# Attention, a routed expert layer and a dense layer in one kernel: another order in the attention, a shorter compaction, x first for the first expert, and other costs in the planner

## The chip, the cores and the metric

The kernel runs on one core of one Trainium2 chip. The metric is the device time of one execution in microseconds. Five engines work in order, each on its own queue: PE multiplies matrices and transposes, DVE, ACT and POOL work elementwise, and SP issues transfers; POOL issues the indirect ones. Data comes from DRAM into on-chip memory, and matmul results lie in PSUM, of which there are eight banks.

## The reference

```python
# 1. attention: B, H, S, D = 4, 8, 768, 64; chunks of 32 queries see 8 memory keys,
#    16 keys to the left, their own 32 and 8 to the right
scores = scale * q_c @ k_full.T
a = exp(scores - max(scores)); a = a / (sum(a) + 1e-09)
out[:, :, c_start:c_end] = a @ v_full
# 2. routed experts: N, D, E, F = 3072, 512, 8, 1024; cap = N // E = 384 tokens each
logits = x @ w_gate
for idx in argsort(-logits.flatten()):       # best pair of token and expert first
    if token is free and expert has room: assigned[tok] = e
for e in range(E):
    out[assigned == e] = max(x[assigned == e] @ w1[e], 0) @ w2[e]
# 3. dense: h = x @ w_in; solu = h * softmax(h); layer norm with gain g_ln; @ w_out
```

All is in float32. Each float32 product of the second and third part is made of three matmuls on a high and a low half (names ending in h and l).

## The kernel before

**Attention** (`attention`, lines 61 to 235) goes over 24 tiles of 128 queries for all 8 heads. Per tile `score` fills `s` with 32 matmuls (the page counts them so, the order lists 16 calls), DVE takes the row maximum `mx`, `less` writes `p` = s - mx, `expo` takes the exponential on ACT, `sums` adds up and inverts on DVE and scales on POOL, `trans` transposes p into `pt`, `pv` multiplies with the values into `o`, which ACT copies to `xs`, and `xtrans` transposes that for the gate. Loads run ahead of it in rings: five tiles of keys `kd` and queries `qt`, four of values `vd`. The keys and values go into block patterns, so the rings are cleared first. `gate` makes the logits `L` of four tiles at a time.

**Routing** (`Route.rounds`, lines 668 to 765) finds one expert per round: `search` finds a threshold in eight counting steps (24 small matmuls `r<-oh,ge`, then `r<-some,ones`, each answered by DVE), then the round picks the expert (`flags`, `es`, `iw`), ranks its tokens (`mk`, `slot`), packs their numbers into `idx` (`compact`, lines 767 to 819: one-hots `ohl` and `rhs`, 24 matmuls, the copy `cc`, four replicating matmuls), and masks the assigned ones in L. Round 0 has nothing beside it; the later ones run beside the experts.

**Experts** (`Experts.run`, lines 1104 to 1187). For each: POOL gathers three x tiles (`xg`) by idx and the weights (`raw`) by `iw`; PE transposes x (`tp<-ident,xg`), ACT and DVE split it into `xh` and `xl`; `g12` makes h = x w1 and y = h w2 in eight steps f of 12 + 12 matmuls; `g3` multiplies with the dense `in` matrix, 72 matmuls, called G3 here; `g4` with `out`, 72 matmuls, G4, one expert later. Beside this, `Fixed` splits the dense weights in chunks of 512 columns (tiles `v`, `e`, `in_h`, `in_l`, `out_h`, `out_l`), on ACT, DVE and POOL.

**What sets the order.** All engines work in program order, and the order is made when the program is built: `Pace` keeps one estimated clock per engine, advanced by `cost` and `charge` for every recorded instruction. The main line of PE work is written straight down; side jobs (routing, splits, chunks) are generators that `tick` resumes when their time has come by these clocks, or, with `yield "spare", "dve"`, when that engine's clock is not ahead of PE's by more than an allowance, less `fit` before another job's due time. So a different cost or `FIT` moves side jobs among the main rows. All instructions are recorded through one helper, so that the profile gives them one line, L398.

Of the kernel before, what the change touches and what calls it, by code (L numbers as in the profile page):

```python
# [42 lines left out]
FIRST_A = 3  # L43
SPARE = 1.27
FIT = 0.34
FIT_OUT = 0.27
# [8 lines left out]
def warm(nc, p, ident, n):  # L55

    for i in range(n):
        nc.tensor.transpose(p[:, i % 4], ident, ident)


def attention(nc, tc, q, kx, vx, wgx, ident, x_dram, L, consts, beside):

    with ExitStack() as ctx:
# [13 lines left out]
        def load_kq(i):  # L77
            if i < NT:
                for h2 in range(2):
                    nc.sync.dma_start(KD[i % AHEAD][h2::2, h2], kx[i, h2])  # L80
                nc.sync.dma_start(QT[i % AHEAD], q[i])
# [6 lines left out]
        for i in range(AHEAD):  # L88
            (nc.gpsimd if i % 2 else nc.vector).memset(KD[i], 0.0)
            if i < AHEAD - 1:  # L90
                (nc.vector if i % 2 else nc.gpsimd).memset(VD[i], 0.0)
# [6 lines left out]
        consts()  # L98

        warm(nc, ps.tile([128, 4, 128], F32, tag="t", name="warm"), ident, 20)  # L100
# [78 lines left out]
        def gate(u, js=range(4)):  # L179
            if js[0] == 0:  # L180
                G[u] = ps.tile([128, 128], F32, tag="t", name="g")
# [5 lines left out]
            if js[-1] == 3:  # L187
                g, G[u] = G[u], wk.tile([128, 128], F32, tag="gs", name="gs", bufs=2)
                nc.scalar.copy(G[u], g)

        def gate_last(i):

            g = ps.tile([128, 4, 128], F32, tag="t", name="g")[:, 0, 0:E]
# [4 lines left out]
        def gate_t(u):  # L198
            g = ps.tile([128, 4, 32], F32, tag="t", name="g")
            nc.tensor.transpose(g, G.pop(u), ident)  # L200
            nc.vector.tensor_scalar(L[:, 4 * u:4 * u + 4, :], g[:, :, 0:E], 0.0, None, op0=ALU.add)

        for i in range(NT + 5):
            n = 0
# [26 lines left out]
            if i > NT:  # L231
                gate_last(i - 5)
            if NT + 1 >= i >= 6 and (i - 6) % 4 == 3:
                gate_t((i - 6) // 4)
            beside(i, 4)


class Pace:
# [61 lines left out]
    def cost(self, eng, op, outs, ins, kw):  # L300
# [3 lines left out]
        if eng == "dve":  # L304
            return n / (1920 if op == "tensor_scalar" else 960) + 0.07
        if eng == "act":
            return n / 1200 + 0.09 + (0.15 if len(outs) > 1 or op == "activation" and n > 512 else 0.0)
        if eng == "pool":
            return n / (480 if op == "tensor_tensor" else 960) + 0.15
        t = (0.108 if op == "transpose" else max(0.03, 0.06 * n / 128) if kw.get("tile_position") else  # L310
             max(0.025, n / 2400 + 0.003))
# [4 lines left out]
    def charge(self, eng, op, args, kw):  # L316
# [8 lines left out]
        if "dma" in op:  # L325
            self.clk[eng] = start + (1.04 if eng == "pool" else 0.05)
# [193 lines left out]
class Route:  # L520
# [6 lines left out]
    def __init__(self, ctx, nc, tc, L, beside):  # L527
# [4 lines left out]
        self.held, self.stage = False, 0  # L532

    def consts(self, ident):
        nc, k = self.nc, self.k
# [8 lines left out]
        self.tri = k.tile([128, 128], F16, name="tri")  # L544
        V.tensor_scalar(self.tri, self.row, col, None, op0=ALU.is_gt)
# [4 lines left out]
        for i in range(3):  # L550
            V.tensor_scalar(self.jtab[:, i], self.jtab[:, 3], float(16 ** (3 - i)), None, op0=ALU.mult)
        off = iota(self.w.tile([128, 8, E], F32, tag="oh", name="off"), [[-15, 8], [0, E]], 0, 1)
        self.own = k.tile([128, 8, E], F16, name="own")
        up = self.w.tile([128, 8, E], F32, tag="rhs", name="up")
        V.tensor_scalar(up, off, 0.0, None, op0=ALU.is_ge)
        V.scalar_tensor_tensor(self.own, off, 15.0, up, op0=ALU.is_lt, op1=ALU.mult)
        V.tensor_tensor(up, self.own, off, op=ALU.mult)
# [707 lines left out]
```

## Time and profile before

| | |
|---|---|
| median of 3 runs | 783.28 us (783.23 to 784.56) |
| the profiled execution | 785.33 us, its span 783.6 us |
| PE busy | 715.6 us, 91% of the span |
| DVE busy | 528.2 us, 67% |
| ACT, POOL busy | 335.9 us, 43%; 199.2 us, 25% |
| chain that ended last | PE 72%, DVE 17%, waits on issue 3%, ACT 3%, DMA 2% |

The span is that of the instructions on the core; the execution's own time is 1.73 us longer. The slices of the page show three stretches: up to 118 us the attention, with PE between six and nine tenths; from 118 to 153 us a stretch in which PE is little used and its granted clock falls to 0.5; and from there on PE at nine tenths. A busy PE can still be slow, since a matmul's duration overlaps the next one's: the distance of two starts says what one costs.

### The profile page before, as it was taken

Reading aid. Unit: us, or ns where it says so; the run is one execution under the profiler, and the core shown is the slowest. Engines: PE = TensorE matmul, PEld = TensorE weight load, DVE = VectorE, ACT = ScalarE, POOL = GpSimd, SP = SyncE. Lnnn points to the kernel's source line nnn. Section 1 sums busy time; section 2 is a strip of 40 time slices with the busy share of each in tenths; the row PEclk is TensorE's granted clock in tenths of the full one; section 3 lists DMA queues with packets and bytes.
Section 4 is the critical chain, followed back from the end, with each engine's and each line's share of the span. In section 5 each row is a group of like instructions: output and inputs, shape, how many; then the busy total and the mean of one; then the engine's idle time right before and its main releaser. Section 6 shows DMA issues by size and latency. Waiting matters only on the chain.

```text
span 783.6 us, 14636 instructions
## 1 busy us (share of the span) xinstructions
PE 715.6 (91%) x5760; PEld 616.5 (79%) x5760; DVE 528.2 (67%) x1434; ACT 335.9 (43%) x646; POOL 199.2 (25%) x263
## 2 busy tenths in 40 slices
PE   6988784499989999999999999999999999999993
PEld 5766674378869978988898789888988898899882
DVE  7788866589997986972897289639964852553150
ACT  1565550234374354432742273237324632563170
POOL 5234530432441134004101420232023211410121
PEclk8999995689999999999999999999999999999997
DMA  7999873532360044004400430152015110600100
GB/s 252 343 323 331 320 286 132 202 103 60 110 227 1 1 162 131 5 1 147 150 1 17 160 120 1 36 181 81 1 55 188 55 40 28 220 10 1 40 14 27
DMA packets 30020, 89.35 MB, mean 114 GB/s; under 512 B 4224, under 2 KB 4352, under 8 KB 29952
## 3 DMA queue, kind: packets, MB, share of 16 engines
q0 software_dynamic: 13056, 46.14, 17.3%
q1 hardware_dynamic: 16896, 42.28, 15.6%
q8 instruction: 45, 0.74, 0.4%
q14 instruction: 23, 0.19, 0.1%
HBM read 75.83 MB, written 12.58 MB: 113 GB/s over the span
## 4 chain that ended last, share of the span: by engine, by line
PE 72%; DVE 17%; issue 3%; ACT 3%; DMA 2%; POOL 1%; POOLq 0%; DVEq 0%; ACTq 0%
PE h L398 32%; PE y L398 16%; PE o L398 15%; PE tp L398 4%; PE r L398 3%; DVE e L398 3%; DVE sum L398 2%; DMA xg<-x_dram,idx 2%; DVE p L398 2%; DVE mx L398 1%; DVE ge L398 1%; ACT p L398 1%; DVE w1l L398 1%; PE xtp L398 1%; PE g L398 1%
## 5 line engine op out<-in xcount | busy, mean ns | idle before, releaser
L398 PE MATMUL y<-hh,w2h 128*128 128x384 f32 x256 | 91.6, 358 | 7.9 <-DVE e L398 7.9
L398 PE MATMUL y<-hl,w2h 128*128 128x384 f32 x256 | 88.3, 345 | 0.0
L398 PE MATMUL y<-hh,w2l 128*128 128x384 f32 x256 | 87.1, 340 | 0.0
L398 POOL DMA_INDIRECT raw<-in_w_dram,iw x64 | 62.3, 974 | 81.7 <-DVE w1l L398 29.8
L398 POOL DMA_INDIRECT out_dram<-ob,idx x24 | 24.3, 1014 | 227.4 <-ACT ob L398 227.0
L398 DVE TENSOR_REDUCE nm<-h 128x1 f32<-128x512 f32 x48 | 33.0, 687 | 72.6 <-PE h L398 72.3
L398 PE MATMUL o<-out_h,lh 128*128 128x512 f32 x192 | 77.2, 402 | 0.0
L398 PE MATMUL h<-in_h,yh 128*128 128x512 f32 x192 | 76.5, 399 | 0.0
L398 PE MATMUL h<-in_l,yh 128*128 128x512 f32 x192 | 76.2, 397 | 0.0
L398 PE MATMUL h<-in_h,yl 128*128 128x512 f32 x192 | 75.9, 396 | 0.0
L398 PE MATMUL o<-out_h,ll 128*128 128x512 f32 x192 | 75.6, 394 | 0.0
L398 PE MATMUL o<-out_l,lh 128*128 128x512 f32 x192 | 75.1, 391 | 0.0
L398 ACT ACTIVATE hh<-h 128x384 fp32r<-128x384 f32 x64 | 31.4, 491 | 90.4 <-PE h L398 77.3
L398 PE MATMUL h<-xh,w1l 128*128 128x384 f32 x256 | 60.1, 352 | 2.5 <-DVE w1l L398 2.4
L398 PE MATMUL h<-xh,w1h 128*128 128x384 f32 x256 | 59.5, 349 | 1.2 <-ACT w1h L398 1.2
L398 ACT CAST w2h<-raw 128x512 fp32r<-128x512 f32 x64 | 39.6, 620 | 48.0 <-PE y L398 43.5
L398 PE MATMUL h<-xl,w1h 128*128 128x384 f32 x256 | 58.1, 346 | 0.0
L398 PEld LDWEIGHTS y<-hh,w2h 128*128 128x128 f32 x256 | 48.2, 188 | 9.8 <-DVE e L398 9.6
L398 DVE TENSOR_TENSOR xl<-tp,xh 128x512 fp32r<-128x512 f32 x24 | 16.6, 690 | 50.2 <-ACT xh L398 35.2
L398 DVE TENSOR_TENSOR w2l<-raw,w2h 128x512 fp32r<-128x512 f32 x64 | 43.8, 685 | 8.7 <-ACT w2h L398 8.7
L398 PEld LDWEIGHTS h<-xh,w1l 128*128 128x128 f32 x256 | 46.6, 195 | 3.3 <-DVE w1l L398 3.2
L398 PEld LDWEIGHTS y<-hl,w2h 128*128 128x128 f32 x256 | 48.5, 189 | 0.2
(194 smaller groups left out, 1603.1 us busy)
## 6 DMA issues: line engine op xcount, KB each, us to landing
vd<-in_vx_dram SPq DMA_DIRECT2D x48, 256.0 KB, 5.3
kd<-in_kx_dram SPq DMA_DIRECT2D x48, 176.0 KB, 5.0
qt<-in_q_dram SPq DMA_DIRECT2D x24, 256.0 KB, 4.9
x_dram<-xs SPq DMA_DIRECT2D x6, 1024.0 KB, 9.8
raw<-in_win_dram SPq DMA_DIRECT2D x8, 512.0 KB, 6.0
raw<-in_wout_dram SPq DMA_DIRECT2D x8, 512.0 KB, 3.7
raw<-in_w_dram,iw POOLq DMA_INDIRECT x64
xg<-x_dram,idx POOLq DMA_INDIRECT x24
```

Source lines behind the costliest of these rows:

```text
L398: return fn(*args, **kw)
```

## The change

In the attention, `sums(i - 1)` moves behind `score(i)` and `less(i)`; `trans(i - 2)` moves to the end of the step for all but the last tiles; `expo(i)` goes behind `pv(i - 3)`; the transposes for the gate get their own PSUM tag; the last three tiles before the final one share one gate; three of the nine clears go to ACT; the queries are loaded ahead of the keys; the 20 transposes that kept PE at work at the head go. The constants of the routing become a side job. In `compact` the two index tables (chunk and lane) become one table of token numbers in float16. For the first expert POOL gathers x behind one weight transfer only, the first w1 split is issued straight away, warm-up matmuls are on float16 ones, and routing of expert 1 is held until x is split. The planner's costs change: 0.16 in place of 0.07 and 0.09 us per instruction on DVE and ACT, 1.25 and 0.35 for an issued transfer, `FIT` 0.62, `FIT_OUT` 0.5.

```diff
-FIT = 0.34
-FIT_OUT = 0.27
+FIT = 0.62
+FIT_OUT = 0.5
...
+        nc.vector.memset(KD[0], 0.0)
+        clear(KD[1])
+        nc.gpsimd.memset(KD[2], 0.0)
...
-        consts()
-
-        warm(nc, ps.tile([128, 4, 128], F32, tag="t", name="warm"), ident, 20)
+        pace.add(consts(), FIRST_C, 0)
...
-            t = ps.tile([128, 4, 128], F32, tag="t", name="xtp")
+            t = ps.tile([128, 4, 128], F32, tag="x", name="xtp")
...
+            if i < NT:
+                s = score(i)
+                less(i, s)
+                load_kq(i + AHEAD)
             n = 0
             for _ in sums(i - 1) if 0 <= i - 1 < NT else ():
                 beside(i, n)
                 n += 1
-            if i < NT:
-                s = score(i)
-                less(i, s)
-                load_kq(i + AHEAD)
-            if 0 <= i - 2 < NT:
+            if i >= NT and i - 2 < NT:
                 trans(i - 2)
-            if i < NT:
-                expo(i)
             beside(i, 3)
             if 0 <= i - 3 < NT:
                 pv(i - 3)
+            if i < NT:
+                expo(i)
...
+            if 2 <= i < NT:
+                trans(i - 2)
             beside(i, 4)
...
-            return n / (1920 if op == "tensor_scalar" else 960) + 0.07
+            return n / (1920 if op == "tensor_scalar" else 960) + 0.16
...
-                while r not in self.idx:
+                while r not in self.idx or self.hold:
                     yield 0.0
...
-        V.scalar_tensor_tensor(am, sl, 32.0, low, op0=ALU.add, op1=ALU.subtract)
-        V.tensor_tensor(am, am, s1, op=ALU.mult)
+        V.tensor_tensor(am, sl, low, op=ALU.subtract)
         yield idle
-        rhs = self.t("rhs", [NT, 2, A], BF)
-        V.tensor_tensor(rhs[:, :, 1], self.atab[:, None, :].to_broadcast([128, NT, A]),
+        rhs = self.t("rhs", [NT, A], F16)
+        V.tensor_tensor(rhs, self.atab[:, None, :].to_broadcast([128, NT, A]),
                         am[:, :, None].to_broadcast([128, NT, A]), op=ALU.is_equal)
         yield idle
-        V.tensor_tensor(rhs[:, :, 0], rhs[:, :, 1], self.cnum[:, :, None].to_broadcast([128, NT, A]), op=ALU.mult)
-        yield idle
-        V.tensor_scalar(rhs[:, :, 1], rhs[:, :, 1], self.col, None, op0=ALU.mult)
+        V.tensor_tensor(rhs, rhs, self.tok[:, :, None].to_broadcast([128, NT, A]), op=ALU.mult)
...
-        self.load_w(0, range(2))
+        self.load_w(0, (0,), (1,))
         self.fixed.hold = True
         while 0 not in self.idx:
             tick()
         self.beside.limit = 0
         self.gather(0)
-        self.load_w(0, (2,))
+        self.load_w(0, (0,), (2,))
+        self.load_w(0, (1, 2))
         self.fixed.hold = False
-        for f in range(2):
-            self.split_w(0, f, (1,))
+        self.split_w(0, 0, (1,), True)
+        p = self.ph.tile([128, 4, 128], F32, tag="h", name="warm")
+        warm(nc, p, self.route.ones, 40)
+        for t in range(TT):
+            self.x_prep(0, t)
+            warm(nc, p, self.route.ones, 5)
+        self.split_w(0, 1, (1,))
         for f in range(2):
             self.split_w(0, f, (2,))
-        warm(nc, self.ph.tile([128, 4, 128], F32, tag="h", name="warm"), self.ident, 25)
-        for t in range(TT):
-            self.x_prep(0, t)
         for t in range(TT):
             self.need("x", 0, t)
+        self.route.hold = False
```

DVE in the attention, before, two tiles in a row (the numbers tell the tiles' buffers apart):

```order
L398 TENSOR_REDUCE mx_529<-s_509 128x8
L398 TENSOR_TENSOR p_531<-s_509,mx_529 128x4x2x64
L398 TENSOR_REDUCE sum_570<-p_531 128x8
L398 TENSOR_SCALAR sum_570<-sum_570 128x8
L398 RECIPROCAL rec_573<-sum_570 128x8
L398 TENSOR_REDUCE mx_593<-s_576 128x8
L398 TENSOR_TENSOR p_595<-s_576,mx_593 128x4x2x64
L398 TENSOR_REDUCE sum_634<-p_595 128x8
```

The same engine after, also two tiles, here with a piece of a weight chunk between them:

```order
L421 TENSOR_REDUCE mx_731<-s_712 128x8
L421 TENSOR_TENSOR p_733<-s_712,mx_731 128x4x2x64
L421 TENSOR_REDUCE sum_738<-p_638 128x8
L421 TENSOR_SCALAR sum_738<-sum_738 128x8
L421 RECIPROCAL rec_741<-sum_738 128x8
L421 TENSOR_SCALAR L_67<-g_771 128x32
L421 TENSOR_SCALAR e_663<-v_662 128x512
L421 TENSOR_REDUCE mx_799<-s_781 128x8
L421 TENSOR_TENSOR p_801<-s_781,mx_799 128x4x2x64
L421 TENSOR_REDUCE sum_806<-p_733 128x8
```

Before, the sum reads the p that was written in the row above it; now it reads the p of the tile before.

DVE at the compaction for expert 1, before; `hl` and `w2l` belong to the h and y of expert 0, `out_l`, `v` to a chunk of the dense weights:

```order
L398 TENSOR_TENSOR ohl<-row,low 128x384 x2
L398 TENSOR_TENSOR w2l<-raw_2625,w2h 128x512
L398 SCALAR_TENSOR_TENSOR out_l<-v,gl,out_h 128x512
L398 CAST cc<-r 128x24
L398 SCALAR_TENSOR_TENSOR v<-v,e 128x512
L398 TENSOR_SCALAR tok<-r 128x3
L398 TENSOR_TENSOR idx_3188<-tok,r 128x3
```

And after; `h_3273` is the last product with the in matrix of expert 0:

```order
L421 TENSOR_REDUCE nm<-h_3273 128x1
L421 TENSOR_TENSOR nm<-nm 128x1
L421 TENSOR_TENSOR ohl<-row,low 128x384
L421 SCALAR_TENSOR_TENSOR out_l<-v,gl,out_h 128x512
L421 SCALAR_TENSOR_TENSOR v<-v,e 128x512
L421 CAST cc<-r 128x12
L421 TENSOR_SCALAR e<-v 128x512
L421 SCALAR_TENSOR_TENSOR e<-raw,e 128x512
L421 TENSOR_SCALAR idx_3383<-r 128x3
```

The idx of expert 1 stood among the splits of expert 0's y stage; now it stands behind the reduction of the last h of its in stage.

PE around the transposes of expert 1's x, before, in the middle of expert 0's in stage:

```order
L398 MATMUL h_3303<-in_h,yh 128x512
L398 MATMUL h_3303<-in_l,yh 128x512
L398 MATMUL h_3303<-in_h,yl 128x512
L398 MATMUL tp<-ident,xg 128x128 x4
L398 MATMUL h_3368<-in_h,yh 128x512
```

And after, behind the end of that stage:

```order
L421 MATMUL r<-rhs,ohl 32x12
L421 LDWEIGHTS rep
L421 MATMUL r<-cc,rep 32x3
L421 MATMUL tp<-ident,xg 128x128 x12
L421 MATMUL h<-xh,w1h 128x384
L421 LDWEIGHTS ge
```

The three groups of transposes stood apart among matmuls with the in matrix; now they stand together, between the compaction's matmuls and the first h of expert 1.

## Rows read from the trace of the kernel before

**Rows 1.** Stages: busy PE, PEld, DVE, ACT, POOL; granted clock, DMA share, GB/s.

```profile
24.47:105.15 80.68, 67.64 (x1492) 51.72 (x1494) 65.62 (x132) 48.35 (x93) 36.16 (x31) 0.98 0.88 309
20.00:95.00 75.00, 64.18 (x1454) 49.39 (x1456) 60.08 (x124) 45.09 (x88) 30.75 (x28) 0.99 0.95 335
153.40:207.45 54.05, 49.03 (x429) 42.37 (x430) 48.87 (x129) 20.78 (x38) 14.70 (x12) 0.91 0.24 73
224.30:306.57 82.27, 78.52 (x444) 67.79 (x443) 66.35 (x196) 42.89 (x84) 20.53 (x30) 0.98 0.21 73
306.57:383.30 76.73, 76.73 (x448) 67.25 (x448) 52.94 (x161) 28.97 (x56) 16.59 (x20) 1.00 0.27 92
```

**Rows 2.** Timeline, DVE: start, duration; maxima of tiles 0, 4, 23; first routing step.

```profile
11.78 0.69 DVE L398 TENSOR_REDUCE mx<-s 128x8 f32<-128x512 f32 x1
...
24.47 0.64 DVE L398 TENSOR_REDUCE mx<-s 128x8 f32<-128x512 f32 x1
...
105.15 0.69 DVE L398 TENSOR_REDUCE mx<-s 128x8 f32<-128x512 f32 x1
...
118.73 0.35 DVE L398 TENSOR_REDUCE m<-L 128x24 f32<-128x192 f32 x1
```

**Rows 3.** Waits of DVE, 24.47 to 105.15 us: total, times, longest.

```profile
DVE sum L398 <- ACT p L398: 7.9, 12, 0.7
```

**Rows 4.** Timeline, PE: the first score.

```profile
6.78 1.93 PE L398 MATMUL s<-kd,qt 128*32 128x128 f32 x32 [0.88 <-DMA qt<-in_q_dram]
```

**Rows 5.** Timeline, DVE: compaction for expert 0.

```profile
141.48 0.29 DVE L398 TENSOR_SCALAR rhs<-rhs,col 128x288 bf16<-128x288 bf16 x1
...
144.88 0.16 DVE L398 TENSOR_TENSOR idx<-tok,r 128x3 int32<-128x3 f32 x1
```

**Rows 6.** Timeline, PE and ACT: the start of expert 0.

```profile
153.40 1.00 PE L398 MATMUL h<-xh,w1h 128*128 128x384 f32 x4 [1.19 <-ACT w1h L398]
...
156.81 0.69 PE L398 MATMUL h<-xh,w1l 128*128 128x384 f32 x1 [2.41 <-DVE w1l L398]
...
160.76 0.49 ACT L398 ACTIVATE hh<-h 128x384 fp32r<-128x384 f32 x1 [4.75 <-PE h L398]
```

**Rows 7.** Timeline, PE: a counting step between h matmuls; two groups without one.

```profile
162.21 0.84 PE L398 MATMUL h<-xh,w1l 128*128 128x384 f32 x2
...
163.67 0.96 PE L398 MATMUL h<-xh,w1l 128*128 128x384 f32 x2
...
199.10 0.86 PE L398 MATMUL h<-xh,w1h 128*128 128x384 f32 x4
...
199.79 0.87 PE L398 MATMUL h<-xh,w1l 128*128 128x384 f32 x4
```

**Rows 8.** Timeline: first and last of 28 routing operations; first in matmul.

```profile
192.46 0.16 DVE L398 SCALAR_TENSOR_TENSOR flags<-r,rev 128x8 f32<-128x8 f32 x1
...
203.19 0.36 DVE L398 TENSOR_TENSOR L<-L,el 128x192 f32<-128x192 f32 x1
...
206.17 0.39 PE L398 MATMUL h<-in_h,yh 128*128 128x512 f32 x1
```

**Rows 9.** Timeline, PE: from expert 0 to 1, and slow h matmuls.

```profile
224.30 0.86 PE L398 MATMUL h<-xh,w1h 128*128 128x384 f32 x4
...
236.25 1.48 PE L398 MATMUL h<-xh,w1h 128*128 128x384 f32 x4
...
238.81 1.02 PE L398 MATMUL h<-xl,w1h 128*128 128x384 f32 x3
```

**Rows 10.** Waits of PE, 224.3 to 306.57 us.

```profile
PE y L398 <- DVE e L398: 2.9, 2, 1.8
```

**Rows 11.** Groups of DVE instructions: busy us, mean ns; idle before.

```profile
L398 DVE TENSOR_REDUCE nm<-h 128x1 f32<-128x512 f32 x48 | 33.0, 687 | 72.6 <-PE h L398 72.3
...
L398 DVE SCALAR_TENSOR_TENSOR out_l<-v,gl,out_h 128x512 fp32r<-128x512 f32 x6 | 5.2, 863 | 0.0
...
L398 DVE TENSOR_TENSOR ohl<-row,low 128x384 bf16<-128x384 bf16 x16 | 8.2, 551 | 0.0
```

More of the change, by code (lines that the diff above doesn't have):

```diff
@@ L52, with warm, attention @@
 SCALE = 1.0 / float(np.sqrt(D))
-def warm(nc, p, ident, n):
+def warm(nc, p, a, n):
     for i in range(n):
-        nc.tensor.transpose(p[:, i % 4], ident, ident)
-def attention(nc, tc, q, kx, vx, wgx, ident, x_dram, L, consts, beside):
+        nc.tensor.matmul(p[:, i % 4], a, a, start=True, stop=True)
+def attention(nc, tc, q, kx, vx, wgx, ident, x_dram, L, consts, pace, beside):
     with ExitStack() as ctx:
@@ L86, in load_v, with clear @@
                     nc.sync.dma_start(VD[i % (AHEAD - 1)][h2::2, h2], vx[i, h2])
[L88 to L91, printed above, removed]
+        zero = keep.tile([128, 1], F32, name="a_zero")
+        nc.vector.memset(zero, 0.0)
+        def clear(t):
+            flat = t.rearrange("p a b c -> p (a b c)") if len(t.shape) == 4 else t.rearrange("p a b c d -> p (a b c d)")
+            nc.scalar.activation(flat, zero.to_broadcast([128, flat.shape[1]]), AF.Copy)
+        nc.vector.memset(KD[0], 0.0)
+        clear(KD[1])
+        nc.gpsimd.memset(KD[2], 0.0)
+        nc.vector.memset(VD[0], 0.0)
+        clear(KD[3])
+        nc.gpsimd.memset(VD[1], 0.0)
+        clear(VD[2])
+        nc.gpsimd.memset(KD[4], 0.0)
+        nc.gpsimd.memset(VD[3], 0.0)
         for i in range(AHEAD):
@@ L177, in attention, with spare, gate @@
         G = {}
-        def gate(u, js=range(4)):
+        def spare():
+            return ps.tile([128, 4, 128], F32, tag="s", name="sp")
+        def gate(u, js=range(4), last=3):
             if js[0] == 0:
-                G[u] = ps.tile([128, 128], F32, tag="t", name="g")
+                G[u] = spare()[:, 0] if last < 3 else ps.tile([128, 128], F32, tag="t", name="g")
             for kc in range(4):
@@ L325, in charge @@
         if "dma" in op:
-            self.clk[eng] = start + (1.04 if eng == "pool" else 0.05)
+            self.clk[eng] = start + (1.25 if eng == "pool" else 0.35)
             n = outs[0].nbytes() if outs[0].space != DRAM else ins[0].nbytes()
@@ L531, in __init__ @@
         self.idx, self.iw = {}, {}
-        self.held, self.stage = False, 0
+        self.held, self.stage, self.making, self.hold = False, 0, True, True
     def consts(self, ident):
@@ L750, in rounds @@
             if r:
-                yield from self.compact(r, s1, sl)
+                yield from self.compact(r, sl)
             else:
-                self.beside.add(self.compact(r, s1, sl))
-                while r not in self.idx:
+                self.beside.add(self.compact(r, sl))
+                while r not in self.idx or self.hold:
                     yield 0.0
@@ L876, in split_w @@
         for n in ns:
-            self.beside.add(parts(n), 0, 0)
+            if now:
+                for _ in parts(n, now):
+                    pass
+            else:
+                self.beside.add(parts(n), 0, 0)
     def gather(self, r):
@@ L1207, in step @@
         beside.tick()
-    attention(nc, tc, q, kx, vx, wg, ident, x_dram, L, lambda: route.consts(ident), step)
+    attention(nc, tc, q, kx, vx, wg, ident, x_dram, L, lambda: route.consts(ident), beside, step)
+    while route.making:
+        beside.tick()
+    beside.limit = 9
     route.open_psum(ctx)
```

87 lines of the change are left out of this document (52 added, 35 removed).

## Prediction

> **What bounds the kernel now.** I read the stage table first, then the chain of waits, then the instructions in order of time around three places, and last the waits by engine. The reader is to see three regimes. From the first score to the first routing step the kernel reads its attention inputs: from tile 4 to tile 23 it takes 80.68 us, in which DVE is busy 65.62 and PE 67.64, and between 20 and 95 us the DMA engines are at a share of 0.95 with 335 GB/s [rows 1]. No engine is full, yet a tile takes (105.15 - 24.47) / 19 = 4.25 us [rows 2]. Part of that is a loop: DVE writes the shifted scores, ACT takes the exponential, and the next thing in DVE's order is the sum of that same tile, which waits 7.9 us in all for ACT [rows 3]. Then routing of expert 0 runs alone, on DVE and PE in turn. From 153.40 us on the experts run, and PE sets the end; but in the first of them DVE is busy 48.87 of 54.05 us, and in the second 66.35 of 82.27, while the third, which has the same matmuls, takes 76.73 [rows 1]. There PE follows DVE. From the third expert on PE is full, and an edit elsewhere is worth nothing there.
>
> **Attention: -8.6 us.** The new order puts the maximum and the subtraction of tile i ahead of the sum of tile i-1, so the sum finds its exponential done; the transposes for the gate get PSUM banks of their own. What a tile costs each engine: DVE 65.62 / 19 = 3.45 us, PE 67.64 / 19 = 3.56 us [rows 1]. For the DMA a tile is 2 x 176 + 256 + 2 x 256 KB by the shapes of kd, qt and vd, and its part of seven weight chunks of 512 KB is 150 KB, 1.30 MB together; 335 GB/s at a share of 0.95 is 353 at a share of 1, so 3.7 us. Nothing can run under 3.7; 4.25 is what there is. I take 3.9, since three engines that are each about nine tenths full seldom meet without a gap, and (4.25 - 3.9) x 19 = 6.6 us. Bounds: 3.7 gives 10.5, 4.25 gives 0. At the head, DVE no longer works through the routing constants before its first maximum: the first score is ready at 8.71 us (6.78 + 1.93), and the maximum starts at 11.78 [rows 2, 4], so up to 3.1 us are given back; the constants go into later gaps beside 24 tiles. Against this stand three clears on ACT, which is idle there, and no warm-up matmuls, so that the first scores run at the 1.93 us of a cold array as they did before, and more of them. I take 2 us, between 3.1 and a loss of 1. The last tile's chain (105.15 to 118.73, 13.6 us [rows 2]) keeps its links; I take nothing for it, between -1 and +1. Together 6.6 + 2.0 = 8.6, between 1 and 13.
>
> **Compaction: -0.8 us.** On the path of expert 0 one addition of 24 elements, one multiply, one pass over 288 elements (0.29) and one conversion go: 0.29 for the pass, and 0.16 for each of the three small ones, as for idx itself: 0.77 [rows 5]. The float16 one-hot has the same elements as before; I take its rows as they are. Bounds 0.4 to 1.2. Nothing hides it: DVE and PE alternate there.
>
> **First expert up to its third matrix: -5.3 us.** Now the x gathers stand ahead of all weights but one on POOL's queue, and routing of expert 1 is held until the three x tiles are split. Before, from the end of idx (144.88 + 0.16 = 145.04) the first h matmul comes 8.36 us later, then waits 2.41 us for w1l, which stands behind ten routing operations, and the first hh is at 160.76, 15.7 us after idx [rows 5, 6]. After, I take 7.8 us to the first h (w1h is cast before the x tiles, which takes away part of its 1.19 us wait). The PE work from there to the first matmul with in_h: 192 matmuls at (199.79 - 199.10) / 4 = 0.173 us are 33.2, and eight counting steps at 1.35 are 10.8: each holds PE from about 162.56 (two matmuls after 162.21) to 163.67, 1.1 us, and 0.25 for its second part [rows 7]. Sum 44.0. DVE has less to do here: 28 routing operations, from the choice of the expert to the mask of L (192.46 to 203.55 before, 7.6 us of their own durations), move behind this stage [rows 8], so 48.9 - 7.6 = 41.3 us, less than PE's 44. I add 4 us for the places where one waits for the other (the first y matmul needs hl, which stands behind the mask of L and two w2l). 7.8 + 44.0 + 4 = 55.8 after idx; before it was 206.17 - 145.04 = 61.1 [rows 5, 8]. Gain 5.3, between 1 and 9.
>
> **The start of the second expert: +13.5 us.** This is what the 28 moved operations cost. Before, idx of expert 1 was ready while y was being made, and the three groups of transposes stood between G3 matmuls; h of expert 1 started at 224.30 without a wait [rows 8, 9]. Now the order has nothing on PE between the last G3 matmul and the transposes but the compaction itself. From the end of G3, one behind the other: the signal 0.2, on DVE the last h's maximum 0.69 and its minimum with the other half 0.2, the second half of the one-hot 0.55, out_l 0.86 and the chunk pass v, which I take alike, 0.86, the copy cc 0.2, PE's four replicating matmuls with their signals 0.5, the rest of two more chunk passes behind cc 0.8, idx 0.16 [rows 5, 11]: 5.0 us. From idx to the first h it took 8.36 us at expert 0, where nothing else was to be done either [rows 5, 6]; I take 8.1. Sum 13.1, and 0.4 for a DVE that is a little late. G3 itself loses three groups of transposes and gains three small matmuls, which I set against each other. Bounds: 9 if DVE is ahead and the gathers land early, 16 if it is late.
>
> The array will have been idle for ten of these microseconds. Before, two waits for DVE of 2.9 us together, 1.8 the longer, are followed by eight h matmuls in 238.81 - 236.25 = 2.56 us, 0.32 each [rows 9, 10], the level of 1.2 GHz instead of 2.4, so 1.2 us lost on eight. The Trainium skill (TensorE: Matmul & The Clock Gate, Part 1) says that the slow clock is the default and only sustained work lifts it; the trace agrees with these 0.32 us against 0.173, and by that rule every one of the first 24 h matmuls could pay 0.17, 4 us. By the row alone it would be 1.2 to 2.5.
>
> **Second expert and the rest: -2.2 and -0.5 us.** The second expert takes 82.27 us before, 5.5 more than the third with the same matmuls [rows 1]; 2.9 of that are the two waits for DVE [rows 10]. DVE goes on with other work during the wait for the gather, so it is less behind afterwards. I take 4.7 off and 2.5 on for the cold start: -2.2, between -5 and +2. For the six later experts the rows keep their kinds and counts and stand a few places elsewhere among full PE rows; -0.5, between -4 and +3.
>
> Sum: -8.6 - 0.8 - 5.3 + 13.5 - 2.2 - 0.5 = -3.9 us on the profiled execution, whose own time is 785.33 us and whose span is 783.6. That execution was 2.05 us over the median of the runs, 783.28, so I set the difference against the median: 779.4.
>
> **Rivals.** *The transfers set the attention's pace.* For it: a share of 0.95 at 335 GB/s [rows 1], which leaves 5% of 75 us, 3.7 us, and a cold array at the start takes some of it. Against it: over all the tiles from 4 to 23 the share is 0.88 at 309 GB/s [rows 1], and the ring holds five tiles. Then attention gives 2 instead of 8.6 and the sum of all other terms, +4.7, wins: +2.7, 786.0, up to 788 if the second expert gains nothing. The point from which it decides: attention has to give 4.7 us, so the first routing operation has to stand before 114.0 us.
>
> *The engines reach the floor and the wait is short.* 3.7 per tile, head at its best, the wait at the boundary 10 us and the first expert at 8: -12.5 - 0.8 - 8 + 10 - 3 - 0.5 = -14.8, 768.5. For it: 7.9 us of pure waiting for ACT go [rows 3]. Against it: DVE's share from tile 4 to 23 is 65.62 / 80.68 = 0.81 [rows 1], and 3.7 us per tile would need 0.93.
>
> *It cancels.* Attention gives 4 to 6 and the boundary takes them: within 1.6 us of 783.3. *The order does not do what it says* would be the wait at the boundary being hidden by something I overlook; it lies in the second rival.
>
> **How the numbers follow.** Forecast 0.42 (its own range 774 to 782), floor rival 0.20, slower rival 0.24, cancelling 0.14. A difference of 0.2%, 1.6 us, is what a measurement can tell: faster 0.62, same 0.14, slower 0.24. The range for 8 in 10 is 769 to 788: the floor rival's middle below, the slower rival with no gain in the second expert above.
>
> **What would show it.** The first routing reduction at 110 us (right from 106 to 114); idx 25.5 us behind it; the first matmul with in_h some 56 us after idx; then a gap on PE of 9 to 16 us that holds only compaction and twelve transposes, ended by the gather; and a granted clock under 1 after it. No gap there, or a first reduction after 116 us, makes the forecast wrong.

## The result: 1.2% slower, and the profile after

The changed kernel takes 792.83 us (790.93 to 795.79, 4 runs), the kernel before 783.84 us beside it on the same chip: a ratio of 1.0117, with a 95% interval of 1.0097 to 1.0136. The forecast was 779.4, so the sign was wrong. The profiled execution has a span of 793.9 us, 10.35 more than before (the medians differ by 9.0). It splits like this, from one landmark to the next:

| stretch | before | after | change | predicted |
|---|---|---|---|---|
| to the maximum of tile 4 | 24.47 | 20.74 | -3.7 | -2.0 (head) |
| tile 4 to tile 23 | 80.68 | 84.47 | +3.8 | -6.6 |
| tile 23 to the first routing step | 13.58 | 18.44 | +4.9 | 0 |
| to idx of expert 0 | 26.15 | 24.25 | -1.9 | -0.8 |
| to the first in matmul | 61.29 | 56.08 | -5.2 | -5.3 |
| to the first h of expert 1 | 18.13 | 31.38 | +13.25 | +13.5 |
| to the first h of expert 2 | 81.27 | 83.10 | +1.8 | -2.2 |
| to the end | 477.99 | 475.45 | -2.5 | -0.5 |

(Here idx is taken at its start. The first h of expert 2 stands at 305.57 before, 1.0 us ahead of the border drawn in [rows 1], and at 318.46 after.) Behind the first routing step the sum of the terms came out, +5.4 for +4.7, though partly by misses that cancel. The attention did not come out: it was to give 8.6 us and took 4.9, and these 13.5 us are nearly the whole miss of 14 between the two sums. The prediction's own sign of being wrong, a first reduction after 116 us, came with 123.65.

The stages of after, in the columns of [rows 1]: tile 4 to 23, the stretch from 20 to 95 us, the gap in front of expert 1, expert 1, and expert 2.

```profile
20.74:105.21 84.47, 66.71 (x1504) 53.02 (x1508) 71.98 (x147) 48.88 (x95) 39.98 (x39) 0.96 0.87 304
20.00:95.00 75.00, 58.01 (x1331) 46.04 (x1323) 63.96 (x136) 43.96 (x85) 34.78 (x34) 0.97 0.93 330
...
221.05:235.36 14.31, 3.98 (x42) 2.59 (x41) 9.06 (x28) 7.83 (x15) 4.49 (x5) 0.58 0.29 92
...
235.36:318.46 83.10, 80.32 (x435) 69.60 (x436) 64.66 (x177) 37.61 (x72) 22.81 (x32) 0.93 0.22 74
318.46:393.50 75.04, 74.85 (x436) 65.47 (x435) 50.41 (x148) 27.61 (x53) 15.74 (x19) 1.00 0.24 82
```

Against [rows 1], the attention's stretch has 6.4 us more of busy DVE (71.98 for 65.62) and is 3.8 us longer. The same points on DVE as in [rows 2] and [rows 5], start and duration:

```profile
8.19 0.69 DVE L421 TENSOR_REDUCE mx<-s 128x8 f32<-128x512 f32 x1
...
20.74 0.69 DVE L421 TENSOR_REDUCE mx<-s 128x8 f32<-128x512 f32 x1 [0.28 <-PE s L421]
...
105.21 0.69 DVE L421 TENSOR_REDUCE mx<-s 128x8 f32<-128x512 f32 x1
...
123.65 0.35 DVE L421 TENSOR_REDUCE m<-L 128x24 f32<-128x192 f32 x1
...
147.90 0.16 DVE L421 TENSOR_SCALAR idx<-r 128x3 int32<-128x3 f32 x1 [0.30 <-PE r L421]
```

The head's gain is there at tile 4 and gone at tile 23. The wait that the new order was to take away did go: DVE's waits between these two tiles, against the 7.9 us of [rows 3]:

```profile
DVE mx L421 <- PE s L421: 3.7, 4, 2.3
...
DVE sum L421 <- ACT p L421: 0.9, 1, 0.9
```

But others grew. DVE's waits together fell only from 10.6 to 8.4 us, and PE's rose from 12.7 to 17.8, most of it for ACT's copy pt of the transposed p; the new order puts that transpose at the end of the step:

```profile
PE o L421 <- ACT pt L421: 13.1, 14, 2.8
```

What came in DVE's time is in the groups of DVE's instructions in the two stretches (busy us, mean ns): first before, from 24.47 to 105.15 us, then after. These are the pieces of the weight chunks that are split beside the attention.

```profile
L398 DVE TENSOR_SCALAR e<-v 128x512 int32<-128x512 int32 x12 | 8.0, 675 | 0.1
L398 DVE SCALAR_TENSOR_TENSOR v<-v,e 128x512 int32<-128x512 int32 x6 | 5.8, 974 | 0.1
L398 DVE SCALAR_TENSOR_TENSOR e<-raw,e 128x512 f32<-128x512 uint32 x6 | 4.8, 800 | 0.1
```

```profile
L421 DVE TENSOR_SCALAR e<-v 128x512 int32<-128x512 int32 x14 | 9.4, 673 | 1.8 <-ACT v L421 1.7
L421 DVE SCALAR_TENSOR_TENSOR v<-v,e 128x512 int32<-128x512 int32 x7 | 8.5, 1215 | 0.2
L421 DVE SCALAR_TENSOR_TENSOR e<-raw,e 128x512 f32<-128x512 uint32 x7 | 6.4, 913 | 0.1
```

All seven chunks now stand between these tiles (28 pieces, 24.3 us); before, 24 pieces of 18.6 us did, and the last four lay behind tile 23, where DVE is busy 7.3 of 13.6 us. And the mean piece is longer. On PE behind tile 23, and at the gap:

```profile
108.70 0.63 PE L421 MATMUL t<-ident,p 128*128 128x128 f32 x4 [1.49 <-DVE p L421]
...
112.45 1.06 PE L421 MATMUL o<-vd,pt 128*32 128x128 f32 x26
115.52 0.42 PE L421 MATMUL o<-vd,pt 128*32 128x128 f32 x6 [2.00 <-issue]
...
203.98 0.40 PE L421 MATMUL h<-in_h,yh 128*128 128x512 f32 x1
...
224.00 0.20 PE L421 MATMUL r<-cc,rep 128*32 128x3 f16 x4 [1.10 <-DVE cc L421]
229.44 2.09 PE L421 MATMUL tp<-ident,xg 128*128 128x128 f32 x8 [5.23 <-DMA xg<-x_dram,idx]
231.90 1.11 PE L421 MATMUL tp<-ident,xg 128*128 128x128 f32 x4 [0.38 <-DMA xg<-x_dram,idx]
235.36 0.66 PE L421 MATMUL h<-xh,w1h 128*128 128x384 f32 x1 [2.34 <-DVE xl L421]
```

PE waits 1.49 us for the p of tile 22 (108.70), stops for 2.00 us in the middle of the values of a tile for nothing that the profile shows, and has the predicted gap of 14.3 us in front of expert 1, ended by the gather.

### The profile page after: what moved, and what is told of

Same layout as the page of the kernel before. It is cut to its first block, busy times and chain, and to the rows that moved or that the text cites. A ratio compares the mean times of both kernels' runs of the same rounds, so it can differ in the third digit from the quotient of the medians.

```text
span 793.9 us, 14632 instructions
## 1 busy us (share of the span) xinstructions
PE 715.5 (90%) x5771; PEld 618.4 (78%) x5771; DVE 525.4 (66%) x1398; ACT 340.1 (43%) x650; POOL 200.4 (25%) x263
## 3 DMA queue, kind: packets, MB, share of 16 engines
q1 hardware_dynamic: 16896, 42.28, 15.5%
## 4 chain that ended last, share of the span: by engine, by line
PE 70%; DVE 11%; issue 8%; DMA 5%; ACT 3%; POOL 1%; SPq 0%; POOLq 0%; DVEq 0%
PE h L421 32%; PE y L421 15%; PE o L421 14%; PE tp L421 3%; PE r L421 3%; DVE e L421 2%; DMA xg<-x_dram,idx 1%; DMA kd<-in_kx_dram 1%; DVE p L421 1%; DVE v L421 1%; DVE sum L421 1%; PE s L421 1%; DVE mx L421 1%; DVE ge L421 1%; DMA qt<-in_q_dram 1%
## 5 line engine op out<-in xcount | busy, mean ns | idle before, releaser
L421 POOL DMA_INDIRECT out_dram<-ob,idx x24 | 24.5, 1019 | 261.2 <-ACT ob L421 260.4
L421 PE MATMUL y<-hh,w2l 128*128 128x384 f32 x256 | 88.7, 346 | 0.0
L421 PE MATMUL o<-out_l,lh 128*128 128x512 f32 x192 | 76.8, 400 | 0.0
L421 ACT ACTIVATE ob<-o,k 128x512 f32<-128x512 f32 x24 | 16.5, 687 | 96.6 <-PE o L421 94.0
L421 PE MATMUL h<-xh,w1l 128*128 128x384 f32 x256 | 57.8, 344 | 0.0
L421 DVE SCALAR_TENSOR_TENSOR hl<-h,hh 128x384 fp32r<-128x384 f32 x64 | 35.5, 555 | 28.5 <-ACT hh L421 28.4
L421 ACT CAST w1h<-raw 128x512 fp32r<-128x512 f32 x64 | 39.7, 620 | 25.8 <-DVE idx L421 25.8
```

Of the source, the lines that this page charges most:

```text
L421: return fn(*args, **kw)
```

## The experiments

Only stages are compared where an edit lies in the attention: the planner's clocks run through the whole program, so such an edit also moves rows in later experts (e9 and e10 below take 76.7 us for experts that take 74.65 in the changed kernel, with the experts' code untouched). One execution of each is traced, and the same rows do not always take the same time: up to the reduction the changed kernel and e7 have the same order on every engine, and reach it at 123.65 and 125.04 us (84.47 and 86.63 us from tile 4 to tile 23); e14 and e15 have the same order there too, with 118.35 and 116.90. So some 2 us between two traces is not shown to be more than scatter. e3, e4, e5, e12 and e13 were executed once each and only their stages are read. "Reduction" is the first routing step, m out of L.

**e1 and e2: the step order alone.** In the first the loop of before is put back into the changed kernel, in the second the new loop into the kernel before (the diff of the change, either way).

> The changed kernel with the step order of before in the attention (sum of tile i-1 ahead of the score of tile i, transposes of p early, exponential ahead of the values); head, gate, costs and experts stay changed. Theory A (the loads set the attention's pace, and what was lost is lost behind the last tile): the maximum of tile 23 stays between 103.5 and 106.5 us (105.2), the first routing reduction comes 2 us earlier, 121.0 to 122.5 instead of 123.65, and the whole run is about 791. Theory B (the new step order itself makes each tile slower): tile 23 at 101 to 102, the reduction at 115 to 117, the whole 784 to 786.

> The kernel before with only the new step order in the attention. Theory A: tile 23 within 1.5 us of 105.15, the first routing reduction 2 to 3 us later than 118.73 (the sum of tile 22 now stands behind the maximum and the subtraction of tile 23), the whole run 785 to 787. Theory B: the reduction at 122 or later, and the whole run 788 or more. The forecast that fell said 112 for the reduction, without the head's 2 us.

e1: reduction at 106.51 us, tile 23 at 92.85, the whole 810.23 us (ratio 1.0338, 1.0316 to 1.0360). e2: tile 23 at 114.26, reduction at 129.63, 796.28 us (1.0160, 1.0136 to 1.0184). Theory A fell in both, and Theory B's numbers for e1 were not met either. But e1 is no clean test: with this loop the planner put not one piece of a weight chunk into the attention (the eight are split later, hence the 810), so that it shows what the chunks cost as much as what the order does. e2 has all 28 pieces, and is 10.9 us behind before.

**e3 and e4: fewer transfers**, in the changed kernel and in the kernel before.

```diff
         def load_v(i):
-            if i < NT:
+            if i < AHEAD - 1:
```

> The changed kernel, which loads values only for the first four tiles of the attention and uses these for all (so its output is another): 10.5 MB of 31.2 fall away, no engine has less to do. Only the time of the attention is read. Theory A: the tiles run at the engines' pace, 3.9 us or less, so tile 23 comes at 8.2 + 23 x 3.9 = 98 us or earlier and the reduction before 116. Theory B: tile 23 within 1.5 us of 105.2 and the reduction within 1.5 of 123.65.

> The kernel before, which also loads values only for the first four tiles (its output is another). Theory A: the stall for keys at 64 us goes, tile 23 comes 3 to 6 us earlier than 105.15, since the loop of subtraction, exponential and sum at 3.1 to 3.6 us per tile remains beside the pieces of the weight chunks; the reduction at 113 to 116. Theory B says the same of this kernel, with which the one above is compared: by A the new order is now ahead of this one by 2 us or more at tile 23, by B it is behind.

e3: tile 23 at 103.34, reduction at 121.36. e4: 103.15 and 116.73. The reductions come 2.3 and 2.0 us earlier for a third of the bytes, no more than the scatter (e15, with the loads and the order of before, has 116.90), and neither theory's numbers came. In e3 the planner also puts the pieces elsewhere. The rival of the prediction (the transfers set the pace) is out, for the orders as they are.

**e5: no chunk in the attention**, against e1, which has none either.

```diff
-CHUNKS_A = 7
+CHUNKS_A = 0
```

> The changed kernel with no weight chunk split in the attention (all eight of the in matrix come behind it, so that the experts are late; only the attention is read). To be set beside the run with the old step order, in which no chunk was split in the attention either and the first routing reduction stood at 106.51 us. Theory C (the new step order itself makes tiles slower, since PE and ACT then wait for each other in a longer chain): reduction at 111 or later. Theory D (the chunks' pieces on DVE are what costs, the step order is worth nothing either way): 105 to 108.5.

Reduction at 108.26, in Theory D's range. The stretch from tile 4 to tile 23 (columns as in [rows 1]), e5 with the new order and then e1 with the old:

```profile
19.86:88.40 68.54, 64.11 (x1504) 51.30 (x1508) 47.92 (x119) 41.55 (x81) 21.54 (x26) 1.00 0.94 326
```

```profile
21.25:92.85 71.60, 66.51 (x1492) 51.97 (x1495) 48.20 (x114) 42.37 (x80) 20.75 (x26) 0.98 0.94 322
```

Without chunks the new order is the faster one by 3.1 us, 3.61 against 3.77 us a tile, not far above the scatter. With them the changed kernel takes 84.47: the seven chunks cost 15.9 us. Behind tile 23 e5 takes 19.9 us, e1 13.7: the last tiles pay 6 us here, 2.0 of them in the stop of PE.

**e6: the new order and the own banks**, in the kernel before.

```diff
-            t = ps.tile([128, 4, 128], F32, tag="t", name="xtp")
+            t = ps.tile([128, 4, 128], F32, tag="x", name="xtp")
```

> The kernel before with the new step order and, as in the changed kernel, an own pair of PSUM banks for the gate's transposes. With the new step order alone the first routing reduction stood at 129.63 us. Theory C: it stays at 126 or later, the run at 792 or more. Rival (what slowed it is only the shared bank, for which PE waited 7.9 us for ACT to empty the transposes): 118 to 121, the run 783 to 786.

Reduction at 120.73, 788.63 us (1.0078, 1.0048 to 1.0108). So 8.9 of e2's 10.9 us came from the shared banks, and Theory C fell, though the run is above the rival's 783 to 786. What is left, 2.0 us, lies behind tile 23 (105.09 to 120.73 is 15.6, before 13.6); from tile 4 to 23 it takes 82.19 us, with all 28 pieces in it (12 of them over 1 us), where before takes 80.68 with 24 (6 over 1 us).

**e7: what makes the gap in front of expert 1.** The cost of a DVE instruction goes back behind the attention; the hold on the routing stays.

```diff
-            return n / (1920 if op == "tensor_scalar" else 960) + 0.16
+            return n / (1920 if op == "tensor_scalar" else 960) + self.dve
...
-    beside.limit = 9
+    beside.limit, beside.dve = 9, 0.07
```

> The changed kernel with its planner's cost of a DVE instruction back at 0.07 us from the end of the attention on (0.16 before it). In the order the compaction for expert 1 then stands in the y stage of expert 0 again, and the three groups of transposes stand apart in its in stage. If that cost makes the gap in front of expert 1: reduction within 1 us of 123.65, no wait of PE for a gather over 1 us there, first h of expert 1 at 222 to 226 instead of 235.36, the first in matmul 1 to 4 us later than 203.98, and the run 781 to 786. If the hold on the routing makes the gap, as the prediction had it: 791 or more.

PE there: the last transposes of expert 1's x, then h with no wait.

```profile
219.57 0.60 PE L421 MATMUL tp<-ident,xg 128*128 128x128 f32 x4
225.62 0.86 PE L421 MATMUL h<-xh,w1h 128*128 128x384 f32 x4
```

First in matmul at 207.51, first h of expert 1 at 225.62, 18.1 us later as before; 785.87 us (1.0024, 0.9998 to 1.0051). The hold alone does not make the gap; it takes that one cost (the cost without the hold was not run). Without the gap the run is level with before although its reduction stands 6.3 us later, at 125.04.

**e8: the old order with chunks** (the planner's allowance raised, so that six chunks come in).

```diff
-SPARE_A = 1.38
+SPARE_A = 3.6
```

> The changed kernel with the old step order in the attention and the planner's allowance there at 3.6 in place of 1.38, so that six weight chunks are split in the attention again (seven in the changed kernel). Theory C: first routing reduction at 111 to 116 us, run 783 to 788. Theory D: 119 or later, and 790 or more.

Reduction at 122.06, 798.96 us (1.0203, 1.0181 to 1.0225). The expectation of Theory C fell: with six chunks the old order is 15.5 us behind e1 too. DVE's pieces take 18.1 us here, no more than before (18.6), so their length does not explain this loss; ACT waits 12.0 us for raw chunks. Where the planner puts the pieces costs as much as the step order.

**e9: does ACT's wait for raw chunks matter?** In the changed kernel ACT stands for 13.3 us in front of the cast v, the first operation on a chunk (10.0 for its transfer, 3.3 more under the name of a kd):

```profile
ACT v L421 <- DMA raw<-in_win_dram: 10.0, 3, 4.1
```

```diff
-            beside.add(fixed.all(0, beside, EVERY_A, 0, CHUNKS_A, 8.0))
+            beside.add(fixed.all(0, beside, EVERY_A, 0, CHUNKS_A, 12.0))
```

> The changed kernel with one number other: a weight chunk's first operation (the cast v on ACT, out of the raw chunk) is planned 12 us after its transfer is issued and not 8. Seven chunks are split in the attention as before. Theory E (ACT works in order and stands still at v until the raw chunk has landed, 13.3 us in four places, 2.6 to 4.1 us each, and the attention stands with it): these waits shrink to under 4 us together, tile 23's maximum comes at 97 to 101 instead of 105.21, the first routing reduction at 115 to 119 instead of 123.65, and the run takes 785 to 789. Theory D2 (DVE's time for the 28 pieces is what bounds, the waits of ACT lie beside it): tile 23 within 2 us of 105.2, reduction 121.5 or later, the run 791 or more.

The waits did go, in ACT's list of waits, and the pieces grew, in DVE's groups from tile 4 to 23:

```profile
ACT v L421 <- DMA raw<-in_win_dram: 0.5, 1, 0.5
```

```profile
L421 DVE TENSOR_SCALAR e<-v 128x512 int32<-128x512 int32 x14 | 11.9, 850 | 0.2
L421 DVE SCALAR_TENSOR_TENSOR v<-v,e 128x512 int32<-128x512 int32 x7 | 10.2, 1463 | 0.2
L421 DVE SCALAR_TENSOR_TENSOR e<-raw,e 128x512 f32<-128x512 uint32 x7 | 8.6, 1222 | 0.1
```

Reduction at 123.03, tile 23 at 107.08; 806.80 us (1.0286). Theory E's numbers fell and D2's held: 12.8 us of ACT's waiting gone gave 0.6 us. But the pieces now take 30.7 us instead of 24.3, so the run does not price the waits by themselves: what they gave may have gone into the pieces.

**e10: the old order for tile 23 alone**, the loop otherwise new.

```diff
+            old = i == NT - 1
-            if i < NT:
+            if i < NT and not old:
                 s = score(i)
...
+            if old:
+                s = score(i)
+                less(i, s)
-            if i >= NT and i - 2 < NT:
+            if (i >= NT or old) and i - 2 < NT:
                 trans(i - 2)
```

> The changed kernel with the old step order for tile 23 alone: the sum of tile 22 ahead of the score of tile 23, and transposes and exponential where they stood. If the new order is what the last tiles pay (the sum of tile 22 waits for the maximum and the subtraction of tile 23, PE for its p): from tile 23's maximum to the first routing reduction 16 to 16.7 us instead of 18.44, and 14 to 14.7 if the stop of PE for 2.0 us in the middle of the values of tile 22 also goes, since another instruction then stands at that place. If the shared last gate is what costs, it stays at 18. The run 1.5 to 4 us under the changed kernel's 792.8.

From tile 23 (106.60) to the reduction (120.26) 13.66 us, the 13.58 of before and better than expected. The same rows of PE as above:

```profile
106.52 0.63 PE L427 MATMUL t<-ident,p 128*128 128x128 f32 x4 [0.96 <-DVE p L427]
...
111.46 1.08 PE L427 MATMUL o<-vd,pt 128*32 128x128 f32 x32
112.47 0.66 PE L427 MATMUL xtp<-ident,xs 128*128 128x128 f32 x4
```

The values of tile 22 run through without the stop of 2.00 us. The whole, 802.42 us (1.0236) where 789 to 791 was expected, is slower by later experts: experts 4 to 6 take 6.6 us more than in the changed kernel.

**e11: e9, e10 and e7 together**, the DVE cost at 0.16 again for experts 2 to 5.

> The changed kernel with the two edits above (12 us, old order for tile 23) and with the planner's cost of a DVE instruction at 0.07 us from the end of the attention on, 0.16 again for experts 2 to 5 only, where the changed kernel takes 74.65 us per expert against 76.4 before. Theory E: reduction at 112 to 116, no gap in front of expert 1, run at 770 to 776, which is faster than before by 1%. Theory D2: reduction at 118 to 121, run at 777 to 782.

Reduction at 125.36, 790.55 us (1.0074, 1.0052 to 1.0096): neither theory's number. Tile 23 stands at 111.70, and experts 4 and 5 take 76.8 and 76.7 us again.

**e12 and e13: a chunk without DVE's four operations, and without POOL's two.**

```diff
-            V.tensor_scalar(ei, vi, -0x80000000, None, op0=ALU.bitwise_and)
+            if m:
+                V.tensor_scalar(ei, vi, -0x80000000, None, op0=ALU.bitwise_and)
...
-                G.tensor_tensor(lo, v, e, op=ALU.add)
+                G.tensor_tensor(lo, v, hi.bitcast(F32), op=ALU.add)
```

In e12 the other three operations get the same condition (m is 0 for the in matrix), and POOL's sum reads another tile, since e is not written. e13 leaves out POOL's two, and the third product of the in matrix reads the high half:

```diff
-            G.tensor_tensor(v if wide else lo, v, hi.bitcast(F32), op=ALU.subtract)
-            if wide:
-                G.tensor_tensor(lo, v, e, op=ALU.add)
...
-                for x, w in ((self.yh, self.in_h), (self.yh, self.in_l), (self.yl, self.in_h)):
+                for x, w in ((self.yh, self.in_h), (self.yh, self.in_h), (self.yl, self.in_h)):
```

> The changed kernel without the four DVE operations of each in-matrix chunk (so the low half is another, and the output too); their transfers, ACT's cast and copy and POOL's two operations stay. Only the attention is read, 123.65 us to the first routing reduction with all of them and 108.26 with no chunk at all. Theory D2 (DVE's own time for the pieces sets the tiles' pace): reduction at 108 to 112. Theory F (what the chunks cost comes from POOL and ACT, whose queues the attention's own rows stand in): 117 or later.

> The changed kernel without POOL's two operations of each in-matrix chunk (the third product of the in matrix reads the high half instead, so the output is another); transfers, ACT's and DVE's parts stay. If the pieces cost what they cost because POOL runs beside them (the same piece takes 0.43 or 1.38 us, 0.69 or 1.45): the 28 pieces take 15.5 to 17.5 us instead of 24.3, and the reduction comes 5 to 9 us earlier, at 115 to 119. If a piece's duration has nothing to do with POOL: 23 to 25 us for the pieces, and the reduction at 122 to 124.

Tile 4 to 23 in e12, then in e13:

```profile
20.54:96.25 75.71, 66.82 (x1504) 53.20 (x1508) 50.36 (x119) 48.66 (x93) 35.83 (x38) 0.95 0.96 340
```

```profile
20.73:101.97 81.24, 67.44 (x1504) 53.66 (x1508) 65.78 (x146) 49.35 (x94) 22.47 (x26) 0.94 0.90 315
```

e12: reduction at 112.19, 0.2 us beyond what D2 expected; the stretch loses 8.8 of the chunks' 15.9 us, and now the DMA engines are at 0.96. e13: reduction at 120.30, the stretch loses 3.2 us, and the pieces take 19.9 us, between the two expectations. So DVE's own pieces are the larger part, POOL's presence a smaller one (3.2 us is little more than the scatter), and what remains (75.71 against 68.54 without chunks) belongs to the transfers, ACT and POOL together; these three were not told apart.

**e14 and e15: the parts that did what was predicted.** e14 is the changed kernel with the attention and the planner's costs of before; e15 adds one line (and a cost that reads it, as in e7).

```diff
+            self.beside.dve = 0.16 if 2 <= r < 6 else 0.07
             self.g12(r, extra)
```

> The changed kernel's compaction and its x first for the first expert, with the attention and the planner's costs of before. From the stages measured: the reduction at 118 to 119.5 as before, 1.9 us gained from there to idx, 1 to 4 us from idx to the first in matmul, no gap in front of expert 1, later experts as before: 777 to 781 us, faster than before by 0.3 to 0.8%. By the theory that the planner's order gives such gains back to DVE in expert 1: 782 to 786.

> As the run above, with the planner's cost of a DVE instruction at 0.16 us for experts 2 to 5 alone. There the changed kernel took 74.65 us per expert for 76.4 before: if that order carries over, 1.7 us less for each of four experts, 771 to 776 us; if its gain hangs on the rest of the changed kernel's order, within 2 us of the run above.

e14: 773.51 us, a ratio of 0.9868 (0.9853 to 0.9882): 1.3% faster than before, and better than expected. e15: 788.79 us (1.0060, 1.0044 to 1.0076), 15.3 us behind e14 and neither of the two expected numbers: experts 3 and 5 take 81.9 and 85.7 us. The changed kernel's 74.65 us per expert hang on the rest of its order. Of e14, the stretches from the first in matmul to the first h of expert 1, and expert 1:

```profile
200.36:219.25 18.89, 18.89 (x114) 14.73 (x113) 16.18 (x38) 11.44 (x25) 13.08 (x12) 1.00 0.68 237
219.25:295.78 76.53, 75.98 (x437) 65.25 (x437) 65.77 (x192) 41.74 (x81) 21.58 (x31) 1.00 0.25 87
```

No gap, and expert 1 takes 76.53 us where before takes 81.27.

## Why the prediction was wrong

**The step that failed is the attention's, in two of its terms.** The first is "I take 3.9, since three engines that are each about nine tenths full seldom meet without a gap, and (4.25 - 3.9) x 19 = 6.6 us". Measured: 84.47 / 19 = 4.45. The wait that the term rested on went (7.9 to 0.9 us), and without chunks the order does give 3.1 us (e5 against e1). But DVE's share was taken as a constant, 3.45 us a tile, from [rows 1]. It is not: where a wait goes, the planner has side work to put. In e6, with the planner's costs of before, the new order alone brings all 28 pieces into the stretch. After, DVE has 71.98 / 19 = 3.79 us a tile, because all 28 pieces, and the routing's constants, now stand in the loop, and because more pieces ran beside POOL. Of the pieces' timeline, after on DVE and then POOL in the same microseconds:

```profile
93.80 0.38 DVE L421 TENSOR_SCALAR e<-v 128x512 int32<-128x512 int32 x1
94.21 1.43 DVE L421 SCALAR_TENSOR_TENSOR v<-v,e 128x512 int32<-128x512 int32 x1
95.68 1.38 DVE L421 TENSOR_SCALAR e<-v 128x512 int32<-128x512 int32 x1
97.09 1.66 DVE L421 SCALAR_TENSOR_TENSOR e<-raw,e 128x512 f32<-128x512 uint32 x1
```

```profile
95.05 1.72 POOL L421 TENSOR_TENSOR v<-v,in_h 128x512 f32<-128x512 f32 x1
96.85 1.35 POOL L421 TENSOR_TENSOR in_l<-v,e 128x512 fp32r<-128x512 f32 x1
```

The same e takes 0.38 and 1.38 us. Over 1 us are 6 of 28 pieces before, 11 after, 17 in e9 and 6 in e13. The Trainium skill (SBUF — State Buffer, Who interferes with whom) says that DVE and GpSimd (POOL) share one pair of ports as an exclusive lock, that a DVE instruction with two inputs in SBUF contends there with a GpSimd one that reads SBUF, and one in its two-port mode too, and that the second to issue is blocked until the first is done. The long pieces here agree with it; the trace shows only that they lie beside POOL's: in before, after, e9 and e13 no piece without a POOL instruction beside it takes over 0.69 us. e13 removes POOL's chunk operations and 4.4 us of the pieces' time, not all of it, since POOL also scales p, and all six of its long pieces lie beside that.

If e1 stands for the old order without chunks (its head and gate are new), the order gave 3.1 us, and the chunks cost 15.9 us where they had cost 80.68 - 71.60 = 9.1. DVE's pieces are 5.7 us of these 6.8 (24.3 for 18.6); e12 shows that DVE's part is more than half of the 15.9, but ACT's waits were not priced apart from it (e8, e9), and that split stays open.

The floor was also a little low: it spread the seven chunks over 24 tiles. With all of them between tiles 4 and 23 a tile moves 340 x 75.71 / 19 = 1.35 MB in e12, which at the prediction's 353 GB/s is an estimated 3.8 us. There, where DVE has room, the DMA engines are at 0.96 and a tile takes 3.98 us, so no run with the chunks in came to the 3.9 that I took for a middle value.

The second is "The last tile's chain (105.15 to 118.73, 13.6 us) keeps its links; I take nothing for it, between -1 and +1". It took 18.44 us, and e10 gives all of that back. The new order puts the sum of tile 22 behind the maximum and the subtraction of tile 23, good while more tiles follow, a delay for the last one: PE's wait of 1.49 us for p is its mark, and in e6 it is 2.0 us alone. The rest is the stop of PE: e9 has the same rows on PE there without the stop, and takes 15.95 us, 2.4 more than before and 2.5 less than the changed kernel. For the whole attention e6 gives the order and the banks 2.0 of the 4.9 us and the stop makes 2.5; no run sets the new costs, gate and constants there apart.

**The head** gave 3.7 instead of 2.0 us at tile 4, and it was worth nothing, because tiles 4 to 23 gave it back.

**Compaction** -1.9 for -0.8: the shorter chain ends 24.25 us after the reduction. e2, e4 and e6, with the chain of before, take 25.0 to 25.3 us where the trace of before takes 26.15 (and e12, with the new chain, 25.3), so the shorter chain itself gave about what was forecast.

**First expert** -5.2 for -5.3, by two misses that cancel. The first h comes 9.5 us after the end of idx, not 7.8, and so 1.2 later than before; from there to the first in matmul it takes 46.4 us, not 48.0:

```profile
157.60 0.97 PE L421 MATMUL h<-xh,w1h 128*128 128x384 f32 x4 [0.40 <-ACT xh L421]
```

**The gap** was right in size, +13.25 for +13.5, and in what ended it, but its cause was named wrongly. The prediction laid it on the hold ("routing of expert 1 is held until the three x tiles are split"), and e7 removes it with the hold in place: it takes the planner's dearer DVE instruction to put the compaction behind G3. That the size fits is in part luck: from the end of G3 to idx it took 4.1 us (5.0 predicted), from idx to h 10.2 (8.1). PE's last 2.34 us there are for xl, and in DVE's order rows of the next counting step (231.81 to 234.53 us) stand in front of the last two xl.

**Second expert** +1.8 for -2.2. Up to its first in matmul it takes 41.0 us where before takes 44.9, so this part of the forecast came. The granted clock is 0.58 in the gap and 0.50 in the 2.6 us behind it, and four of the first twelve h matmuls take 1.28 us (237.19 to 238.47), 0.32 each; from 240.84 us on four take 0.70. For twelve that is an estimated 1.8 us lost, within the 1.2 to 2.5 of the row; the 4 us for 24 matmuls had no row behind its count. The loss lies in the out stage, 24.5 us for 18.8: PE waits for ACT's out_h, which the forecast did not have, and the granted clock falls a second time.

```profile
PE o L421 <- ACT out_h L421: 2.8, 1, 2.8
```

```profile
300.00:305.00 5.00, 2.79 (x6) 1.91 (x7) 2.73 (x7) 2.72 (x5) 4.26 (x8) 0.68 0.01 3
305.00:310.00 5.00, 5.00 (x18) 4.00 (x17) 0.00 (x0) 0.48 (x1) 3.70 (x6) 0.64 0.50 152
```

e14, without a gap and a cold start, shows the 4.7 us that the term had counted as a gain (81.27 to 76.53).

**The slower rival** (786 to 788) had the sum right in form: all other terms win once the attention gives less than 4.7 us, decided at a reduction after 114.0. Its mechanism, the transfers, is not what decided (e3, e4), and no case had the attention lose.

## What to carry to other kernels

An engine's busy share beside a loop that also feeds side work is no constant: before pricing a wait that goes, ask which rows the planner will put into it, and what they run beside. A reordering that helps a steady loop by putting older work behind newer has to be priced at the last pass on its own. And where a change has parts that can be read stage by stage, keep those that did what they should: compaction and x first alone make 773.5 us of 783.2. A stage that is read from one trace of each kernel is known no better than the same rows repeat, here 1.4 to 2.2 us.

## What the hardware showed that was not expected

PE stopped for 2.00 us in the middle of one tile's matmuls, at the same instruction in the changed kernel (113.51 to 115.52), in e5 (96.61 to 98.61), in e7 (114.90 to 116.90) and in e13 (110.18 to 112.17). The DMA engines are full in all four (a share of 1.02 to 1.03). Just before the stop, at 113.33 in the changed kernel, one packet of 16 KB starts on q8, whose 45 packets go in step with PE's instructions; from the view of DMA queues, after, between 113.3 and 114.4 us:

```profile
q8 instruction: 1, 0.02, 5.5%
```

In all four this packet starts 0.2 to 0.25 us before the stop. e3 and e9 have the same order on PE up to there and run on, and in them a q8 packet started 5.0 and 3.9 us before that instruction, at 108.25 and 111.03. In e9, the matmuls of tile 22's values:

```profile
114.24 1.08 PE L421 MATMUL o<-vd,pt 128*32 128x128 f32 x32
```

The Trainium skill (Runtime: NRT & Kernel Launch, Instruction fetch mechanics) has instructions streamed in blocks of 16 KiB and the crossing mostly hidden. That agrees with the other packets of the changed kernel, beside which PE has no such stop; this one started late, and the order alone does not decide it, since e3 and e9 run on. Why it was fetched late is open.
